# A linear-attention and token-mixer kernel: state packed without its zero blocks, crossbar transposes on another queue and for fewer batches

## The chip, the cores and the metric

The kernel runs on one core of a Trainium2 chip. Five engines take part, each with its own in-order instruction stream: PE (TensorE, matmuls), DVE (VectorE), ACT (ScalarE), POOL (GpSimd) and SP (SyncE, which here only issues transfers). The metric is the device time of one execution in microseconds. Before the change the median of three runs is 233.55 us (233.35 to 233.89).

## The reference, cut to what matters

Batch 4, 8 heads, 768 time steps, head size 48. A gated recurrence gives y, and y, with the heads side by side (384 wide), goes through a token mixer and a channel mixer:

```python
f = 1 / (1 + exp(-f_logit))
for t in range(768):
    state = f[:, :, t, :, None] * state + einsum('bhd,bhe->bhde', k[:, :, t], v[:, :, t])
    y[:, :, t] = einsum('bhd,bhde->bhe', q[:, :, t], state)
x = heads_side_by_side(y)                     # (4, 768, 384)
h = relu(x.T @ w_tok1) @ w_tok2               # over the 768 steps, hidden 256
u = x + h.T
out = u + relu(u @ w_ch1) @ w_ch2             # over the 384 channels, hidden 1536
```

## The kernel before, in words

**Attention.** Each batch b is worked in three blocks d of 256 steps, and each block in two chunks e of 128 steps; below "(b,d)" is one block. The recurrence is done chunk by chunk: within a chunk the sum of log gates is taken by matmuls (`cums`), its exponentials multiply q and k (`gate`, four DVE instructions a block), the gated q and k are transposed so that the head dimension lies on the partitions, `score` forms q times k for 8 heads, `mk` masks it on DVE, `av` multiplies with v, and `qs` adds what q reads from the state of the chunk before. `ds` forms the chunk's contribution to the state (k times v), DVE adds and scales the state (`s_add`, `s_mul`, `s_first`), and POOL casts it to bf16 (`bdc`). Two heads share 128 partitions, at rows 0 to 47 and 64 to 111. Before the change `ds` multiplies both heads of a pair against both v's, so half of each 96-column result is unwanted; DVE and POOL pick the wanted halves with two instructions each, and the bf16 state is a block-diagonal tile with zeros beside each head's block, so that one 128-row matmul of `qs` serves a pair. ACT then copies y out of PSUM (`xev`, L510), POOL or ACT casts it for the mixer.

**Mixing.** Per batch there are 12 matmuls of 384 columns in `tok1`, 12 in `tok2`, 72 in `ch1` (L595) and 72 in `ch2` (L626). ACT and DVE take the results out of PSUM (relu, L606 and L608; additions, L554 and L638), and SP stores the output in two transfers per block.

**Two ways to transpose.** Batch 0 transposes q, k and u with matmuls against an identity (L408, L566) and copies the results out of PSUM on ACT or DVE. Batches 1 to 3 use crossbar transposes by DMA, from SBUF to SBUF, two per block for q and k (L421) and one per block for u (L581). They are issued from ACT's stream.

**What sets the order.** A planner in the kernel (class `Planner`) gives each operation an engine, a cost and a priority, and walks a made-up clock; the engines then run the instructions in the order it found. So an edit of costs or priorities rearranges all five streams. Four PSUM slots (pool "PP", two banks each) are shared by everything that PE writes. Each of f, q, k and v has five load buffers. The transfers that SP and ACT issue share eight completion semaphores in rotation in program order, so a transfer waits until the one that is eight places earlier has ended, whichever queue that one is on. POOL loads the weights; a small POOL write into a load buffer (`gate_w`) holds the loads of batch 1 back until the weights are issued.

Of the kernel before, what the change touches and what calls it, by code (L numbers as in the profile page):

```python
# [11 lines left out]
ALU = mybir.AluOpType  # L12
# [22 lines left out]
class Planner:  # L35
# [23 lines left out]
    def run(self):  # L59
# [25 lines left out]
        free, pipe = {}, 0.0  # L85
        slot_of, last = {}, {}
        order = []
        while ready:
# [27 lines left out]
            if o.xfer is not None and o.xfer < 0:  # L116
                begin = st + occ + 0.5
                end = begin - (2 if pipe > begin else 1) * o.xfer + 1.2
                pipe = max(pipe, begin) - o.xfer
            elif o.xfer is not None:  # L120
                begin = max(st + occ + 0.5, pipe)
                pipe = begin + o.xfer
                end = pipe + 1.2
# [14 lines left out]
            for u, issued in users.get(id(o), []):  # L138
                waiting[id(u)] -= 1
                ready_at[id(u)] = max(ready_at[id(u)], st + occ if issued else end + SEM)  # L140
                if waiting[id(u)] == 0:
                    ready.append(u)
# [12 lines left out]
def kernel(  # L155
# [22 lines left out]
    XB_FROM = 1  # L178
# [40 lines left out]
    bd_tiles = [st([128, HP, 2 * D], BF16, f"state_bd{i}") for i in range(3)]  # L219
# [10 lines left out]
    def consts():  # L230
# [16 lines left out]
        for t in st_tiles + bd_tiles:  # L247
# [3 lines left out]
    LD_ISSUE, ROW = 0.8, 0.019 / 16  # L251
# [21 lines left out]
    def weight(nm, pieces, prio, after):  # L273
# [3 lines left out]
        P.op(nm, {"POOL": (1.2 * len(pieces), 0)}, [], [nm], fn, prio, after, xfer=w_mb[nm] / 0.38)  # L277
# [5 lines left out]
    for kt in range(2):  # L283
        P.value(f"w2s{kt}", f"w2s{kt}", "z")
    P.op("w2l", {"POOL": (2.4, 0)}, [], ["w2s0", "w2s1"], lambda: [nc.gpsimd.dma_start(
        out=P[f"w2s{kt}"], in_=moe_w_tok2[128 * kt:128 * kt + 128]) for kt in range(2)], -898, ["~w1"],
        xfer=w_mb["w2"] / 0.38)
    P.op("w2", {"DVE": (1.0, 0.1)}, ["w2s0", "w2s1"], ["w2"], lambda: [nc.vector.tensor_copy(
        w_tok2[:, kt].rearrange("r c (two p) -> r c p two", two=2),
        P[f"w2s{kt}"].rearrange("r (c p two) -> r c p two", p=64, two=2)) for kt in range(2)], -898)  # L290
    for nm, dst, src, pr, dep in (("wc1", w_ch1, moe_w_ch1, -897, "w2l"),
                                  ("wc2", w_ch2, moe_w_ch2, -896, "wc1")):
# [3 lines left out]
         lambda: nc.gpsimd.memset(P["gw"][0:1, 0, 0, 0:1], 0.0), -895, ["~wc2"])  # L296
# [14 lines left out]
    def attention(b, d):  # L311
        i, pr = f"{b},{d}", 100 * b + 20 * d
# [36 lines left out]
        flex = {"DVE": dve_t(384), "POOL": pool_t(384, True)} if b == 0 else {"POOL": pool_t(384, True)}  # L349
# [35 lines left out]
        def vcast():  # L385
# [4 lines left out]
            nc.gpsimd.tensor_copy(o[64:128, 0], x[0:64, 1])  # L390
            nc.gpsimd.tensor_copy(o[0:64, 2], x[64:128, 0])
        P.op(f"U{i}", {"POOL": (2.5, 0.1)}, [f"v{i}"], [f"U{i}"], vcast, pr + 1)
# [315 lines left out]
```

## Time and profile before

| | before |
|---|---|
| median of the runs | 233.55 us (233.35 to 233.89) |
| the profiled execution | 232.6 us, of which the span in the profile is 230.7 us |
| busy in the span | PE 172.3 us (75%), DVE 145.1 (63%), ACT 90.4 (39%), POOL 84.0 (36%) |
| DMA, share of 16 engines | loads and stores on SP's queue 46.0%, crossbar transposes on ACT's queue 19.2%, weights on POOL's queue 8.1% |
| mean granted PE clock | 0.931 |
| last copy of y out of PSUM (L510) starts, batches 0 to 3 | 44.9, 93.7, 139.9, 181.9 |

Times below are microseconds from the start of the span. A row such as "L454 DVE TENSOR_TENSOR AmT<-pp,msk ... x24 | 28.9, 1220" is a group of instructions: 24 of them, 28.9 us in all, 1220 ns in the mean. [...] A row named "ACTq" or "SPq" is the engine's queue issuing transfers; it does not count as busy.

### The profile page before, as it was taken

What the parts mean: (1) busy time and instruction counts of PE and PEld (TensorE: products, weight loads), DVE (VectorE), ACT (ScalarE), POOL (GpSimd) and SP (SyncE); (2) the same over time, 40 slices, a digit from 0 to 9 for tenths busy, and PEclk for the clock granted to TensorE, in tenths of its full rate; (3) what the DMA queues carried; (4) which work ended last, traced back from release to release, by engine and by line L of the source; (5) the groups of instructions that cost most, each with busy time, mean ns of one, the idle gap of its engine ahead of it and who ended that gap; (6) DMA issues with size and microseconds to landing.
All of it is one profiled execution on the core that took longest, in us unless ns stands there. A gap on an engine that the chain in (4) does not pass through costs nothing.

```text
span 230.7 us, 3882 instructions
## 1 busy us (share of the span) xinstructions
PE 172.3 (75%) x1514; PEld 101.9 (44%) x1514; DVE 145.1 (63%) x221; ACT 90.4 (39%) x130; POOL 84.0 (36%) x134
## 2 busy tenths in 40 slices
PE   0455726585976859948828999929998999799990
PEld 0243424343443435623514556514554656456550
DVE  4699897549893976938837855908876516124211
ACT  4754505286437816423224267211244512244000
POOL 2279942177745286900546626104302101000000
PEclk9999999999795999995965999988999999999998
DMA  7999999999897999979990330693435004711052
GB/s 170 261 261 231 214 203 236 263 260 265 142 257 175 264 207 194 239 120 236 178 230 0 45 49 0 71 183 67 107 81 78 4 0 80 161 24 44 1 138 68
DMA packets 82642, 33.48 MB, mean 145 GB/s; under 512 B 76608, under 2 KB 82240, under 8 KB 82624
## 3 DMA queue, kind: packets, MB, share of 16 engines
q1 hardware_dynamic: 53376, 23.60, 46.0%
q10 hardware_dynamic: 26208, 6.49, 19.2%
q0 software_dynamic: 3040, 3.15, 8.1%
q8 instruction: 12, 0.20, 0.3%
q14 instruction: 6, 0.05, 0.1%
HBM read 25.17 MB, written 4.72 MB: 130 GB/s over the span
## 4 chain that ended last, share of the span: by engine, by line
PE 41%; DVE 19%; DMA 15%; ACT 9%; issue 8%; ACTq 4%; POOL 1%; SPq 0%; DVEq 0%; POOLq 0%
PE pp L595 15%; PE pp L626 12%; DVE qkh L398 7%; DMA qkT<-qkh 6%; DVE AmT L454 4%; ACTq L421 4%; PE pp L548 3%; DMA q_ld<-in_q_dram 3%; DMA out_dram<-xu 3%; PE pp L528 2%; PE pp L451 2%; DVE state L493 2%; DMA uT<-u_bf 2%; ACT xu L510 2%; ACT f_ld L346 2%
## 5 line engine op out<-in xcount | busy, mean ns | idle before, releaser
L595 PE MATMUL pp<-uT,w_ch 128*128 128x384 bf16 x288 | 58.6, 348 | 5.9 <-ACT zT L606 2.2
L626 PE MATMUL pp<-w_ch,zT 128*128 128x384 bf16 x288 | 57.2, 331 | 2.1 <-ACT xu L510 1.9
L595 PEld LDWEIGHTS <-w_ch 128*128 128x128 bf16 x288 | 28.0, 103 | 26.9 <-issue 11.0
L606 ACT ACTIVATE zT<-pp 128x768 bf16<-128x768 f32 x31 | 24.7, 813 | 32.3 <-PE pp L595 27.4
L626 PEld LDWEIGHTS <-zT 128*128 128x128 bf16 x288 | 27.0, 99 | 19.9 <-issue 3.7
L454 DVE TENSOR_TENSOR AmT<-pp,msk 128x1024 bf16<-128x1024 f32 x24 | 28.9, 1220 | 9.7 <-PE pp L451 9.4
L506 POOL CAST state_bd<-state 48x192 bf16<-48x192 f32 x40 | 15.8, 396 | 34.4 <-DVE state L496 27.5
L608 DVE TENSOR_SCALAR zT<-pp 128x768 bf16<-128x768 f32 x17 | 16.3, 957 | 15.3 <-PE pp L595 11.7
L638 DVE TENSOR_TENSOR xu<-xu,pp 128x768 f32<-128x768 f32 x12 | 11.4, 949 | 19.0 <-PE pp L626 19.0
L510 ACT COPY xu<-pp 128x768 f32<-128x768 f32 x12 | 9.6, 799 | 29.2 <-PE pp L469 13.7
L554 DVE TENSOR_TENSOR xu<-xu,pp 128x768 f32<-128x768 f32 x12 | 11.2, 952 | 13.6 <-PE pp L548 13.6
L451 PE MATMUL pp<-qkT 48*128 48x128 bf16 x192 | 10.7, 252 | 10.8 <-ACT xu L510 4.2
L398 DVE TENSOR_TENSOR qkh<-q_ld,G 128x384 bf16<-128x384 f32 x24 | 15.1, 670 | 4.3 <-ACT G L377 4.3
L462 PE MATMUL pp<-v_bf,AmT 128*128 128x48 bf16 x192 | 9.9, 194 | 10.6 <-DVE AmT L454 10.6
L398 DVE TENSOR_TENSOR qkh<-k_ld,Gi 128x384 bf16<-128x384 f32 x24 | 17.7, 776 | 0.0
L302 POOL CAST x_bf<-xu 128x768 bf16<-128x768 f32 x10 | 8.5, 846 | 25.3 <-ACT xu L510 22.6
L548 PE MATMUL pp<-h1T,w_tok 128*128 128x384 bf16 x48 | 12.9, 432 | 4.2 <-ACT h1T L533 4.2
L350 DVE TENSOR_TENSOR Pf<-f_ld 128x384 f32<-128x384 f32 x12 | 9.3, 788 | 9.7 <-ACT f_ld L348 6.4
L528 PE MATMUL pp<-x_bf,w_tok 128*128 128x384 bf16 x48 | 13.3, 372 | 2.8 <-POOL x_bf L302 1.8
L462 PEld LDWEIGHTS <-AmT 128*128 128x128 bf16 x192 | 7.9, 103 | 15.5 <-DVE AmT L454 14.3
L451 PEld LDWEIGHTS <-qkT 48*128 48x128 bf16 x192 | 7.2, 110 | 16.2 <-issue 8.7
L388 POOL CAST v_bf<-v_ld 64x768 bf16<-64x768 f32 x12 | 11.4, 946 | 8.2 <-DMA v_ld<-in_v_dram 4.0
(72 smaller groups left out, 230.4 us busy)
## 6 DMA issues: line engine op xcount, KB each, us to landing
f_ld<-in_f_logit_dram SPq DMA_DIRECT2D x12, 384.0 KB, 6.2
q_ld<-in_q_dram SPq DMA_DIRECT2D x12, 384.0 KB, 6.2
k_ld<-in_k_dram SPq DMA_DIRECT2D x12, 384.0 KB, 6.0
v_ld<-in_v_dram SPq DMA_DIRECT2D x12, 384.0 KB, 6.1
out_dram<-xu SPq DMA_DIRECT2D x24, 192.0 KB, 3.0
w_ch<-in_moe_w_ch_dram POOLq DMA_DIRECT2D x2, 1152.0 KB, 16.8
w_tok<-in_moe_w_tok_dram POOLq DMA_DIRECT2D x2, 192.0 KB, 6.6
zT<-in_moe_w_tok_dram POOLq DMA_DIRECT2D x2, 192.0 KB, 6.6
```

The lines of the kernel that those rows point to most:

```text
L398: nc.vector.tensor_tensor(gated(z, nm, j), x[:, j], gg[:, j], ALU.mult)
L451: nc.tensor.matmul(A[:, par, hp], lhsT=qkT(1, hp, e, rows), rhs=qkT(0, hp, e, rows), start=True, stop=True)
L454: P.op(f"mk{ic}", {"DVE": dve_t(1024)}, [f"A{ic}"], [f"Am{ic}"], lambda ic=ic: nc.vector.tensor_tensor(P[f"Am{ic}"], P[f"A{ic}"].rearrange ...
L462: nc.tensor.matmul(y[:, h], lhsT=P[f"Am{ic}"][:, (h % 2) * 4 + h // 2, :], rhs=vb[:, h], start=(h == 0), stop=(c == 0 and h == H - 1), ski ...
L506: nc.gpsimd.tensor_copy(P[f"bd{ic}"][r, :, cl], P[f"st{ic}"][r])
L510: lambda: nc.scalar.copy(P[f"x{i}"], P[f"yc{b},{2 * d}"][:, :, 0:DM]), pr + 2)
L528: nc.tensor.matmul(pm[:, rt, 0:DM], lhsT=w_tok1[:, kt, rt * 128:(rt + 1) * 128], rhs=P[f"xb{b},{kt // 2}"][:, kt % 2], start=(kt == 0), st ...
L548: nc.tensor.matmul(pm[:, s, 0:DM], lhsT=w_tok2[:, kt, tt, :], rhs=P[f"h1{b}"][:, kt, :], start=(kt == 0), stop=(kt == 1))
L595: nc.tensor.matmul(pm[:, th, 0:384].rearrange("p (a t) -> p a t", t=128), lhsT=w_ch1[:, kt, cc * 128:(cc + 1) * 128], rhs=uT[:, 3 * th:3 * ...
L606: nc.scalar.activation(o, x, AF.Relu)
L608: nc.vector.tensor_scalar(o, x, 0.0, None, ALU.max)
L626: nc.tensor.matmul(pm[:, s, 0:DM], lhsT=P[f"z{b},{cc}"][:, tt * 128:(tt + 1) * 128], rhs=w_ch2[:, cc, :], start=(cc == 0), stop=(cc == NCC ...
```

## The change

- `ds` forms each head by itself: a 64-column half of the gated k against that head's 48 columns of v, its result on the 64 partitions of that head. That makes 32 matmuls a block where there were 16, and a state result without unwanted halves. DVE adds and scales the state with one 128-partition instruction where two of 48 partitions were needed, and POOL casts it with one. The block-diagonal tile and its zeros go.
- `qs` reads the compact state head by head: eight matmuls of 48 rows and 48 columns a chunk where there were four of 128 rows and 96 columns. y lies in PSUM sorted by head parity (one bank for even heads, one for odd), and `xev` puts the heads in order when it copies.
- Batch 1 now transposes on PE as batch 0 does; only batches 2 and 3 use the crossbar. Those transposes are issued from SP instead of ACT.
- The cast of v is split in two operations, and in batch 0 ACT may take the second. In batch 0 the copies of transposed q and k are on ACT alone. The rearranging copy of `w_tok2` (L288) may go to POOL, with a later priority. The second channel weight is loaded only after the first k of batch 1 has arrived (`gate_2`), and the loads of batch 1 no longer wait for its issue.
- The planner's costs for loads, weights and transposes are altered, and attention gets a priority number that is 70 lower, which is earlier. In the new order 342 of the 672 mixer matmuls stand behind the last state read, in the old 255.

**The SP stream at the loads of batch 3.** Names: `qkT` is the transposed pair q and k, `qkh` the gated ones, `xu` the output. Before:

```order
L258 DMA f_ld_73<-in_f_logit_dram 128x8x96
L258 DMA f_ld_72<-in_f_logit_dram 128x8x96
L258 DMA q_ld_77<-in_q_dram 128x8x96
L258 DMA k_ld_82<-in_k_dram 128x8x96
L258 DMA v_ld_90<-in_v_dram 128x8x96
L258 DMA f_ld_75<-in_f_logit_dram 128x8x96
L258 DMA q_ld_79<-in_q_dram 128x8x96
L258 DMA k_ld_84<-in_k_dram 128x8x96
L645 DMA out_dram<-xu_121 64x2x384 x2
```

and now:

```order
L259 DMA f_ld_74<-in_f_logit_dram 128x8x96
L259 DMA f_ld_75<-in_f_logit_dram 128x8x96
L432 DMA_TRANSPOSE qkT_108<-qkh_105 128x16x64 x2
L259 DMA q_ld_79<-in_q_dram 128x8x96
L432 DMA_TRANSPOSE qkT_107<-qkh_106 128x16x64 x2
L259 DMA k_ld_82<-in_k_dram 128x8x96
L654 DMA out_dram<-xu_121 64x2x384 x2
L259 DMA v_ld_89<-in_v_dram 128x8x96
L259 DMA f_ld_72<-in_f_logit_dram 128x8x96
L654 DMA out_dram<-xu_122 64x2x384 x2
```

The transposes of batch 2, each pair waiting for DVE's gated q and k, now stand between the loads of batch 3: ten of the twelve loads come behind the first of them.

**The DVE stream in batch 0**, from the gates of block (0,0) to those of (0,1). Before:

```order
L302 CAST qkT_107<-pp_152 128x2x8x64
L489 TENSOR_TENSOR state_116<-pp_154,glast_113 48x192 x2
L350 TENSOR_TENSOR Pf_92<-f_ld_74 128x384
L372 TENSOR_TENSOR pp_153<-pp_153,f_ld_73 128x384
L454 TENSOR_TENSOR AmT_110<-pp_155,msk 128x1024
L454 TENSOR_TENSOR AmT_111<-pp_152,msk 128x1024
L355 TENSOR_TENSOR Plo_95<-Pf_92,Phi_94 128x8x48
L398 TENSOR_TENSOR qkh_105<-q_ld_78,G_101 128x8x48 x2
```

and now:

```order
L375 TENSOR_TENSOR pp_153<-pp_153,f_ld_73 128x384
L507 TENSOR_TENSOR state_116<-pp_155,glast_113 128x192
L504 TENSOR_TENSOR state_116<-state_116,pp_155 128x192
L507 TENSOR_TENSOR state_116<-state_116,glast_113 128x192
L467 TENSOR_TENSOR AmT_110<-pp_154,msk 128x1024
L467 TENSOR_TENSOR AmT_111<-pp_155,msk 128x1024
L353 TENSOR_TENSOR Pf_92<-f_ld_74 128x384
L408 TENSOR_TENSOR qkh_105<-q_ld_78,G_101 128x8x48 x2
```

The copy of the transposed q has left DVE for ACT, the state of both chunks is done ahead of the masks, and each of its steps is one instruction.

**The ACT stream around the third batch's first mixing step** (`h1T`, the relu of `tok1`). Before:

```order
L379 ACTIVATE Gi_104<-pp_153 128x768
L381 ACTIVATE glast_114<-pp_153 128x8
L421 DMA_TRANSPOSE qkT_107<-qkh_106 128x16x64 x2
L421 DMA_TRANSPOSE qkT_108<-qkh_105 128x16x64 x2
L533 ACTIVATE h1T_132<-pp_154 128x768
L557 CAST u_bf_136<-xu_122 128x768
L581 DMA_TRANSPOSE uT_137<-u_bf_136 128x6x128
```

and now:

```order
L382 ACTIVATE Gi_103<-pp_155 128x768
L542 ACTIVATE h1T_132<-pp_152 128x768
L615 ACTIVATE zT_143<-pp_153 128x768
L517 COPY xu_122<-pp_154 128x2x8x48
L384 ACTIVATE glast_114<-pp_152 128x8
```

No transfer is issued from ACT any more. The core of the diff:

```diff
-            if o.xfer is not None and o.xfer < 0:
-                begin = st + occ + 0.5
-                end = begin - (2 if pipe > begin else 1) * o.xfer + 1.2
-                pipe = max(pipe, begin) - o.xfer
+            if o.xfer is not None and e == "POOL":
+                sw = max(st + occ + 1.5, sw) + o.xfer
+                pipe = max(pipe, st + occ) + o.xfer
+                end = sw + 1.0
             elif o.xfer is not None:
...
+                pipe = max(st + occ + 0.5, pipe) + o.xfer
+                free[e] = max(free[e], pipe - 4.5)
+                end = pipe + 1.0
...
-    XB_FROM = 1
+    XB_FROM = 2
...
-    bd_tiles = [st([128, HP, 2 * D], BF16, f"state_bd{i}") for i in range(3)]
+    bd_tiles = [st([128, HP, D], BF16, f"state_bf{i}") for i in range(3)]
...
-    LD_ISSUE, ROW = 0.8, 0.019 / 16
+    LD_ISSUE, ROW = 1.1, 0.0235 / 16
...
-    P.op("w2", {"DVE": (1.0, 0.1)}, ["w2s0", "w2s1"], ["w2"], lambda: [nc.vector.tensor_copy(
-        w_tok2[:, kt].rearrange("r c (two p) -> r c p two", two=2),
...
+    P.op("w2", {"DVE": (0.6, 0.1), "POOL": (1.6, 0.1)}, ["w2s0", "w2s1"], ["w2"], lambda e: [cast(
+        e, w_tok2[:, kt].rearrange("r c (two p) -> r c p two", two=2),
...
-                                  ("wc2", w_ch2, moe_w_ch2, -896, "wc1")):
+                                  ("wc2", w_ch2, moe_w_ch2, -896, "gate_2")):
...
-         lambda: nc.gpsimd.memset(P["gw"][0:1, 0, 0, 0:1], 0.0), -895, ["~wc2"])
+         lambda: nc.gpsimd.memset(P["gw"][0:1, 0, 0, 0:1], 0.0), -896.5, ["~wc1"])
+    P.op("gate_2", {"POOL": (0.1, 0.1)}, ["k1,0"], [],
+         lambda: nc.gpsimd.tensor_copy(gate_t, P["k1,0"][:, 0, 0, 0:1]), -896.2)
...
-        i, pr = f"{b},{d}", 100 * b + 20 * d
+        i, pr = f"{b},{d}", 100 * b + 20 * d - 70
...
+        P.op(f"V{i}", {"POOL": (1.02, 0.1), "ACT": (0.74, 0.12)} if b == 0 else {"POOL": (1.02, 0.1)}, [f"v{i}"],
+             [f"V{i}"], vshift, pr + 1.5)
...
-                P.op(f"ev{z}{i}", {"ACT": act_t(1024), "DVE": dve_t(1024)}, [f"T{z}{i}"],
+                P.op(f"ev{z}{i}", {"ACT": act_t(1024)} if b == 0 else {"ACT": act_t(1024), "DVE": dve_t(1024)},
...
-                P.op(f"xb_t{i},{e}", {"ACT": (0.8, 0)}, [f"qh{i}", f"kh{i}"], [f"qkT{i},{e}"],
-                     lambda e=e: nc.scalar.dma_start_transpose(
+                P.op(f"xb_t{i},{e}", {"SP": (1.5, 0)}, [f"qh{i}", f"kh{i}"], [f"qkT{i},{e}"],
+                     lambda e=e: nc.sync.dma_start_transpose(
                          P[f"qkT{i}"][:, 1024 * e:1024 * (e + 1)].rearrange("p (n t) -> p n t", t=64),
...
         def ds():
...
-                        nc.tensor.matmul(P[f"dS{i}"][:, e, hp * 2 * D:(hp + 1) * 2 * D], lhsT=kblk(r, j, hp),
-                                         rhs=P[f"U{i}"][r, e + j, hp * 2 * D:(hp + 1) * 2 * D],
-                                         start=(j == 0), stop=(j == 1), skip_group_check=True)
...
+                        kb = kblk(r, j, hp)
+                        for par in range(2):
+                            h = 2 * hp + par
+                            nc.tensor.matmul(P[f"dS{i}"][64 * par:64 * par + 64, e, hp * D:(hp + 1) * D],
+                                             lhsT=kb[:, 64 * par:64 * par + 64],
+                                             rhs=P[f"U{i}"][r, e + j, h * D:(h + 1) * D],
+                                             start=(j == 0), stop=(j == 1), skip_group_check=True)
...
+            def yv(h, e=e, ic=ic):
+                o = e * HP * D + (h // 2) * D
+                return P[f"ya{ic}"][:, h % 2, o:o + D]
...
-                for hp in range(HP):
-                    nc.tensor.matmul(y[:, hp], lhsT=qkT(0, hp, e), rhs=bd[:, hp, :],
-                                     start=False, stop=(hp == HP - 1), skip_group_check=True)
...
+                s_ = P[f"bd{b},{c - 1}"]
+                for h in range(H):
+                    hp, r = h // 2, slice(64 * (h % 2), 64 * (h % 2) + D)
+                    nc.tensor.matmul(yv(h), lhsT=qkT(0, hp, e, r), rhs=s_[r, hp, :], start=False, stop=True,
+                                     skip_group_check=True)
...
             def s_add(ic=ic, dsv=dsv):
-                for r, cl in half:
-                    nc.vector.tensor_tensor(P[f"st{ic}"][r], P[f"st{ic}"][r], dsv()[r, :, cl], ALU.add)
...
+                nc.vector.tensor_tensor(P[f"st{ic}"], P[f"st{ic}"], dsv(), ALU.add)
...
-                for r, cl in half:
-                    nc.gpsimd.tensor_copy(P[f"bd{ic}"][r, :, cl], P[f"st{ic}"][r])
...
+            P.op(f"bd{ic}", {"POOL": (0.36, 0.1)}, [f"st{ic}"], [f"bd{ic}"],
+                 lambda ic=ic: nc.gpsimd.tensor_copy(P[f"bd{ic}"], P[f"st{ic}"]), pr + 1)
...
-                P.op(f"uT{i}", {"ACT": (1.0, 0)}, [f"ub{i}"], [f"uT{i}"],
-                     lambda i=i, p=p: nc.scalar.dma_start_transpose(
+                P.op(f"uT{i}", {"SP": (1.5, 0)}, [f"ub{i}"], [f"uT{i}"],
+                     lambda i=i, p=p: nc.sync.dma_start_transpose(
```

76 lines of the change are left out of this document (35 added, 41 removed).

## The prediction

> **What bounds the kernel now.** I read the busy time by stretches first, then the chain of waits, then single streams. The stretches end about where the attention of each batch ends (the table above has when the last copy of y out of PSUM starts):
>
> ```profile
> core 0: us, PE busy (x) PEld busy (x) DVE busy (x) ACT busy (x) POOL busy (x), PEclk, DMA share, GB/s
> 3.00:45.00 42.00, 22.32 (x250) 15.15 (x250) 33.81 (x51) 17.41 (x26) 21.44 (x31) 1.00 1.24 241
> 45.00:94.00 49.00, 37.18 (x341) 20.41 (x341) 36.59 (x52) 30.96 (x47) 30.92 (x45) 0.90 1.10 218
> 94.00:140.00 46.00, 35.49 (x321) 20.70 (x320) 30.38 (x45) 16.39 (x25) 18.92 (x29) 0.81 0.67 133
> 140.00:182.00 42.00, 35.84 (x353) 21.04 (x351) 28.45 (x45) 13.90 (x22) 9.50 (x19) 0.96 0.46 81
> ...
> 182.00:231.00 49.00, 41.51 (x254) 24.55 (x252) 14.06 (x15) 10.43 (x13) 1.66 (x2) 0.98 0.26 61
> ...
> sum 179.00, PE 130.83 PEld 77.29 DVE 129.23 ACT 78.67 POOL 80.78; mean PE 32.71 PEld 19.32 DVE 32.31 ACT 19.67 POOL 20.20
> ```
>
> (The last row sums the first four.) DVE is the busiest in the first stretch (33.81 of 42 us, 80%), 75% in the second, 66% and 68% in the third and fourth; PE's time in the later ones is swollen by a granted clock of 0.81 to 0.96. No engine is full: what paces these 179 us is handing work from engine to engine, with DVE's work (129.2 us, 72%) as the nearest floor. What interrupts the handing on is in the chain:
>
> ```profile
> 80.54 8.19 DMA qkT<-qkh
> 107.16 5.27 DMA qkT<-qkh
> 212.97 11.71 PE pp L626 x72
> 224.78 0.95 DVE xu L638
> ```
>
> Crossbar transposes stand in it for 8.19 and 5.27 us at a time. The last two rows show another regime: after the attention, PE runs dense matmuls at 11.71 / 72 = 0.163 us each, and 6.0 us pass between its end (224.68) and the span's end at 230.7. ACT's own stream shows what issuing the transposes costs, before the third batch's relu of the token mixer:
>
> ```profile
> 145.47 7.67 ACTq L421 DMA_TRANSPOSE qkT<-qkh  x4
> 153.18 0.81 ACT L533 ACTIVATE h1T<-pp 128x768 bf16<-128x768 f32 x1 [7.68 <-issue]
> L421 ACTq DMA_TRANSPOSE qkT<-qkh x18: 1257/1758/3676, 57.6 to 172.7; - x18
> L581 ACTq DMA_TRANSPOSE uT<-u_bf x9: 1225/1228/2539, 111.3 to 194.9; - x9
> ```
>
> ACT stands for 7.68 us while four transposes are issued; at the medians the 27 take 18 x 1.758 + 9 x 1.228 = 43 us of its stream, beside its 90.4 us of work. And SP's loads wait for those transposes through the shared completion semaphores:
>
> ```profile
> SPq L258 <- DMA qkT<-qkh: 27.2, 5, 7.5
> q10 hardware_dynamic: 26208, 6.49, 19.2%
> ```
>
> 27.2 us in five waits; and the transposes' queue fills 16 engines for 19.2% of 230.7, 44 us.
>
> **The change, term by term.** The end is the time at which DVE gets through the last mask of the attention, then the last state read, then the dense matmuls behind it, then the tail. On DVE, and for what ACT takes over:
>
> ```profile
> L454 DVE TENSOR_TENSOR AmT<-pp,msk 128x1024 bf16<-128x1024 f32 x24 | 28.9, 1220 | 9.7 <-PE pp L451 9.4
> L608 DVE TENSOR_SCALAR zT<-pp 128x768 bf16<-128x768 f32 x17 | 16.3, 957 | 15.3 <-PE pp L595 11.7 <-ACT xu L510 3.5
> L638 DVE TENSOR_TENSOR xu<-xu,pp 128x768 f32<-128x768 f32 x12 | 11.4, 949 | 19.0 <-PE pp L626 19.0
> L493 DVE TENSOR_TENSOR state<-state,pp 48x192 f32<-48x192 f32 x32 | 11.2, 349 | 3.5 <-PE pp L430 1.8 <-POOL state_bd L506 1.0
> L496 DVE TENSOR_TENSOR state<-state,glast 128x192 f32<-128x192 f32 x16 | 6.6, 413 | 0.3
> L489 DVE TENSOR_TENSOR state<-pp,glast 48x192 f32<-48x192 f32 x8 | 2.8, 352 | 0.9 <-PE pp L430 0.7
> L288 DVE COPY w_tok<-zT 128x768 bf16<-128x768 bf16 x2 | 4.4, 2388 | 0.0
> L302 DVE CAST qkT<-pp 128x1024 bf16<-128x1024 f32 x3 | 3.7, 1220 | 1.5 <-PE pp L408 1.5
> 179.32 1.23 DVE L454 TENSOR_TENSOR AmT<-pp,msk 128x1024 bf16<-128x1024 f32 x1
> L300 ACT CAST qkT<-pp 128x1024 bf16<-128x1024 f32 x3 | 3.0, 1012 | 11.1 <-PE pp L408 11.1
> L606 ACT ACTIVATE zT<-pp 128x768 bf16<-128x768 f32 x31 | 24.7, 813 | 32.3 <-PE pp L595 27.4 <-DVE pp L372 4.6 <-PE pp L626 0.3
> ```
>
> - State: 56 instructions, 11.2 + 6.6 + 2.8 = 20.6 us, become 36 of 128x192. The 48-row ones have the same 192 elements on a partition and take 0.349, the 128-row ones 0.413 in the mean; I take 0.35 (the two of the first kind are one each now), 12.6 us: -8.0 (bound -5.7).
> - The copy of `w_tok2` goes to POOL: -4.4.
> - Casts of transposed q and k: three before, two now: -1.2.
> - Relus on DVE: 17 before, 9 now, ACT takes the others: -8 x 0.957 = -7.7. Copies of transposed u: one before, two now, +0.95.
>
> Together -20.3. Behind the last mask stood 14.1 us of DVE's work (the row from 182 on); in the new order 13 instructions of some 0.95 stand there, 12.4 us. So DVE has 129.2 - 20.3 + 1.7 = 110.6 us to do up to its last mask.
>
> How fast it gets through: 72% over the 179 us. I take 75%, the share of the second stretch. For a higher one: the first stretch had 80%; ACT loses 43 us of issuing and does some 14 us more work (eight relus of 0.81, seven casts of about 1.0, smaller pieces both ways), so 133 us of its stream become about 105; batch 1's transposes cost a few us on PE and ACT instead of landing times. For a lower one: the leaner DVE leaves more of the pace to the others, and PE gets more to do. Both ends go into the range: 70% and 82%.
>
> PE's additions, from its stream among dense matmuls:
>
> ```profile
> 111.44 0.52 PE L430 MATMUL pp<-v_bf,qkh 64*128 64x96 bf16 x16
> 111.89 0.66 PE L626 MATMUL pp<-w_ch,zT 128*128 128x384 bf16 x3
> 163.90 0.33 PE L469 MATMUL pp<-state_bd,qkT 128*128 128x96 bf16 x4
> 164.07 0.65 PE L626 MATMUL pp<-w_ch,zT 128*128 128x384 bf16 x3
> 159.23 0.40 PE L451 MATMUL pp<-qkT 48*128 48x128 bf16 x8
> 159.56 1.15 PE L626 MATMUL pp<-w_ch,zT 128*128 128x384 bf16 x6
> 165.48 0.33 PE L362 MATMUL pp<-Phi,tri 128*128 128x384 bf16 x1
> 166.01 0.65 PE L626 MATMUL pp<-w_ch,zT 128*128 128x384 bf16 x3
> 162.17 0.36 PE L462 MATMUL pp<-v_bf,AmT 128*128 128x48 bf16 x8
> 162.37 0.65 PE L626 MATMUL pp<-w_ch,zT 128*128 128x384 bf16 x3
> L430 PEld LDWEIGHTS <-qkh 64*128 64x128 bf16 x192 | 5.4, 103 | 8.1 <-DVE qkh L398 6.0 <-issue 1.8 <-DVE state L489 0.3
> ```
>
> Sixteen `ds` matmuls cost 111.89 - 111.44 = 0.45 us, 28 ns each; four `qs` cost 0.17; eight 48-column `av` cost 0.20, 25 ns each; eight `score` 0.33; a block's `cums` 0.53. A 64x64 tile with 48 columns was never run, so I bound it: nothing added if four tiles overlap fully; 32 x 28 ns = 0.9 us, +0.45 a block, if each is issued like a present one; 32 x 103 ns = 3.3 us, +2.85, if each waits for its whole weight load. I take +0.45, the row it is nearest to. `qs`: eight at 25 ns and 0.2 for entering and leaving the half-height array (0.09 us passes between two dense matmuls and the 111.44 row) is 0.4, +0.23 for each of 20. Twelve blocks and 20 reads: 5.4 + 4.6 = 10 us. Batch 1's 66 transposes (48 of q and k, 18 of u) have a third of a dense matmul's columns, 0.054 us each: 3.6.
>
> Up to the last state read PE then has 330 mixer matmuls (counted in the new order) at 0.163, 53.7 us; the attention as it was, 12 x (0.45 + 2 x 0.33 + 2 x 0.20 + 0.53) + 20 x 0.17 + 3.6 for batch 0's transposes = 31.5; and these 13.6. That is 98.8 us from its first matmuls at about 8, 69% of the time that DVE sets. Covered; with the upper bound it isn't (rival 2).
>
> POOL loses half of its 40 casts of state, some 8 us, and gains the `w_tok2` copy: between 2 x 0.85 us (its cast of x, as many elements) and the 2 x 2.39 that DVE took; it lies in the first stretch, where POOL is busy for half the time, and costs up to 3 us if a state cast waits behind it. SP gets the transposes: see the first rival.
>
> **The sum.** 3.0 (start of the stretch) + 110.6 / 0.75 = 147.5, so the last mask ends at 150.5 instead of 180.6 (the row at 179.32). The last state read follows 1.1 us later, as before. Behind it stand 342 mixer matmuls in the new order, 255 in the old (attention has moved ahead of them): 342 x 0.1626 = 55.6. Tail 6.0. Span 213.2. The same sum for the kernel before, 180.6 + 1.1 + 41.5 + 6.0 = 229.2, is 1.5 short of 230.7, so the method is good to a few us. The median of the runs is 233.55, 2.85 above the profiled span: **216 us**.
>
> **Rivals.**
> 1. *Transposes queue behind loads on SP.* Now ten of batch 3's twelve loads come behind batch 2's first transposes, and these wait for DVE's gates. Each block of batch 2 may have to let the loads ahead of it land, and PE, which runs in order, stands for it. A load's median to landing:
>
> ```profile
> q_ld<-in_q_dram SPq DMA_DIRECT2D x12, 384.0 KB, 6.2
> ```
>
>    Three blocks: 18.6 us, span 231.8, time 234.7, about the old time. For it: the 27.2 us above show that SP's waits were already of that kind. Against it: the transfers need no longer be shared with batch 1's transposes (a third of 44 us), and in the new order the gates of (2,0) stand 16 rows of DVE ahead of the mask that needs their transposes.
> 2. *Column tiles are slow, the change is slower.* With 103 ns for each `ds` pair and 103 for each `qs` pair, PE gets 12 x 2.85 + 20 x 0.65 = 47 us instead of 10, so 136 us up to the last state read. At 80% that is 8 + 170 = 178, plus 55.6 and 6.0: 239.6, time 242.5. It decides once PE's work passes 0.8 x 143 = 115 us, that is some 70 ns for a `ds` pair. Against it: the 25 to 28 ns rows, where weight loads of 103 ns overlap freely.
>    [...] No run so far shows a column tile. [...]
> 3. *Everything flows.* Without ACT's stalls PE's clock stays full and DVE reaches 82%: 3.0 + 134.9 + 62.7 = 200.6, time 203.5. For it: PE's low clock follows its stalls. Against it: even the first stretch, without crossbar or mixer, had 80%.
>
> **How the numbers follow.** The forecast has 0.64; its own range goes from 82% to 70% of DVE, 203 to 226. Rival 1 has 0.16 (spread around the old time), rival 2 0.10, rival 3 0.10. The range takes in the forecast, rival 1's lower two thirds and half of rival 3: 203 to 233. A measurement of this kernel can tell about 0.2%, 0.5 us. Faster: 0.64 + 0.10 + 0.4 x 0.16 = 0.80; within 0.2%: 0.03; slower 0.17.
>
> **What would show it.** Last copy of y of batch 0 near 38 and of batch 3 near 151 instead of 44.9 and 181.9; DVE busy some 125 us in all; `ds` with 32 matmuls in about 0.9 us among dense ones; no transposes on ACT; about 62 us between the last state read and the end. Wrong: SP waits in front of transposes with PE idle behind them (rival 1), `ds` at 2 us or more (rival 2), or a DVE share below 66%.

## The result

The changed kernel takes 210.78 us in the median of four runs (209.39 to 211.04); the kernel before took 233.72 beside it (233.35 to 235.90). The ratio is 0.8989, with a 95% interval of 0.8921 to 0.9057: faster, by 23 us. The forecast was 216.0, the range 203 to 233. The profiled execution took 211.04 us, its span is 209.3.

The page of the changed kernel: busy time of the engines, one row of its queues, and the chain's shares by engine.

```profile
PE 168.3 (80%) x1852; PEld 103.4 (49%) x1852; DVE 128.6 (61%) x188; ACT 104.5 (50%) x147; POOL 80.5 (38%) x117
...
q1 hardware_dynamic: 70848, 27.93, 65.3%
...
PE 54%; DVE 27%; ACT 8%; issue 6%; DMA 2%; POOL 1%; DVEq 0%; POOLq 0%; ACTq 0%
```

Transfers held 15% of the chain before and ACT's queue 4%; now it is 2% and nothing. The transposes share one queue (q1) with the loads. The table of stretches of the changed kernel (columns as in the prediction; 147.70 is where the last state read starts):

```profile
3.00:147.70 144.70, 112.39 (x1506) 69.76 (x1507) 114.63 (x161) 81.47 (x119) 76.39 (x104) 0.96 0.96 189
147.70:209.00 61.30, 55.90 (x351) 33.49 (x350) 12.24 (x13) 21.70 (x27) 2.48 (x3) 0.98 0.28 62
...
3.00:41.40 38.40, 22.09 (x318) 14.34 (x318) 28.36 (x38) 20.44 (x31) 20.49 (x24) 1.00 1.17 239
41.40:79.70 38.30, 30.40 (x420) 19.37 (x420) 29.81 (x45) 29.98 (x44) 21.05 (x30) 0.96 0.97 195
79.70:105.20 25.50, 19.94 (x263) 12.27 (x261) 23.84 (x31) 11.45 (x19) 19.28 (x28) 0.97 0.95 195
105.20:123.30 18.10, 15.60 (x190) 9.32 (x189) 13.87 (x20) 8.69 (x14) 8.62 (x13) 0.85 1.00 188
123.30:148.00 24.70, 24.66 (x326) 14.69 (x325) 18.76 (x27) 11.19 (x17) 6.95 (x11) 1.00 0.61 94
```

DVE does 114.63 us of work in 144.70, 79% (before 129.23 in 178.6, 72%). PE is full from 123.3 on (24.66 of 24.70); before that it stands for 32 of 120.3 us. Of the marks that the prediction named: batch 0's last copy of y starts at 41.40 (38 foreseen), the last state read of batch 3 is over at 147.85 (the copy of y behind it, foreseen near 151, starts at 154.67, since ACT's copy before it waits 9.2 us for a store to free its buffer, and ACT then waits 5.5 us more for an addition on DVE; PE has no gap from that), DVE is busy for 128.6 us (some 125), and 61.5 us lie between the last state read and the end (62).

Single streams of the changed kernel on PE: a block's chunk states (`ds`, L444) and the last state reads (L485) among dense matmuls.

```profile
130.92 0.44 PE L444 MATMUL pp<-v_bf,qkh 64*64 64x48 bf16 x32
131.29 1.39 PE L557 MATMUL pp<-h1T,w_tok 128*128 128x384 bf16 x7
...
147.35 0.36 PE L478 MATMUL pp<-v_bf,AmT 128*128 128x48 bf16 x8
147.65 0.27 PE L485 MATMUL pp<-state_bf,qkT 48*128 48x48 bf16 x8
147.85 4.40 PE L635 MATMUL pp<-w_ch,zT 128*128 128x384 bf16 x26
```

Thirty-two column-tiled matmuls (64 rows by 64 columns each) take 131.29 - 130.92 = 0.37 us from their row's start to the next row's (the row's own 0.44 runs into the next), 12 ns each; the sixteen before took 0.45. Eight `av` and eight `qs` take 0.30 + 0.20, where eight `av` and four `qs` took 0.20 + 0.17.

And one place where the change costs something: the rearranging copies of the second token weight on POOL, DVE beside them, and the gates by group, with what PE waited for them.

```profile
27.64 7.05 POOL L305 COPY w_tok<-zT 128x768 bf16<-128x768 bf16 x2
...
27.11 2.36 DVE L467 TENSOR_TENSOR AmT<-pp,msk 128x1024 bf16<-128x1024 f32 x2
29.39 0.34 DVE L504 TENSOR_TENSOR state<-state,pp 128x192 f32<-128x192 f32 x1
29.65 4.83 DVE L408 TENSOR_TENSOR qkh<-k_ld,Gi 128x384 bf16<-128x384 f32 x2
...
L408 DVE TENSOR_TENSOR qkh<-k_ld,Gi x24: 543/773/3515, 11.9 to 137.9; 128x384 bf16<-128x384 f32 x24
...
PE pp L444 <- DVE qkh L408: 4.9, 4, 3.1
```

Two gates take 4.83 us, one of them 3.515 instead of 0.773 (the median); the masks in the same window keep their 1.18. PE stands 3.1 us for that gate, the longest of its four such waits.

### The profile page after: what moved, and what is told of

It is laid out like the page before. It is cut to its first block, busy times and chain, and to the rows that moved or that the text cites. A ratio compares the mean times of both kernels' runs of the same rounds, so it can differ in the third digit from the quotient of the medians.

```text
span 209.3 us, 4507 instructions
## 1 busy us (share of the span) xinstructions
PE 168.3 (80%) x1852; PEld 103.4 (49%) x1852; DVE 128.6 (61%) x188; ACT 104.5 (50%) x147; POOL 80.5 (38%) x117
## 4 chain that ended last, share of the span: by engine, by line
PE 54%; DVE 27%; ACT 8%; issue 6%; DMA 2%; POOL 1%; DVEq 0%; POOLq 0%; ACTq 0%
PE pp L635 20%; PE pp L604 18%; DVE qkh L408 11%; DVE AmT L467 5%; PE pp L537 3%; PE pp L557 3%; ACT G L380 2%; DVE Pf L353 2%; DVE state L507 2%; DMA f_ld<-in_f_logit_dram 2%; PE pp L478 2%; PE pp L464 2%; PE pp L418 1%; PE pp L444 1%; DVE xu L563 1%
## 5 line engine op out<-in xcount | busy, mean ns | idle before, releaser
L604 PE MATMUL pp<-uT,w_ch 128*128 128x384 bf16 x288 | 51.7, 330 | 1.6 <-ACT Gi L382 0.8
L635 PE MATMUL pp<-w_ch,zT 128*128 128x384 bf16 x288 | 51.6, 333 | 0.4 <-DVE xu L563 0.4
L615 ACT ACTIVATE zT<-pp 128x768 bf16<-128x768 f32 x39 | 31.5, 812 | 27.9 <-DVE xu L647 17.3
L408 DVE TENSOR_TENSOR qkh<-k_ld,Gi 128x384 bf16<-128x384 f32 x24 | 21.3, 926 | 0.0
L517 ACT COPY xu<-pp 128x768 f32<-128x768 f32 x12 | 9.5, 795 | 21.8 <-PE pp L485 12.6
L408 DVE TENSOR_TENSOR qkh<-q_ld,G 128x384 bf16<-128x384 f32 x24 | 17.3, 759 | 1.9 <-ACT G L380 1.8
L514 POOL CAST state_bf<-state 128x192 bf16<-128x192 f32 x20 | 7.8, 388 | 27.1 <-DVE state L507 27.0
L418 PE MATMUL pp<-ident,qkh 128*128 128x128 bf16 x96 | 10.5, 264 | 4.4 <-DVE qkh L408 3.8
L380 ACT ACTIVATE G<-pp 128x768 bf16<-128x768 f32 x12 | 9.8, 813 | 6.9 <-DVE pp L375 6.9
L303 ACT CAST qkT<-pp 128x1024 bf16<-128x1024 f32 x10 | 10.1, 1010 | 5.5 <-PE pp L418 5.5
L444 PE MATMUL pp<-v_bf,qkh 64*64 64x48 bf16 x384 | 6.4, 199 | 7.0 <-DVE qkh L408 4.9
L305 POOL CAST v_bf<-v_ld 64x384 bf16<-64x384 f32 x20 | 11.6, 579 | 1.0
```

Of the source, the lines that this page charges most:

```text
L305: (nc.vector if e == "DVE" else nc.gpsimd).tensor_copy(o, x)
L380: P.op(f"G{i}", {"ACT": act_t(768)}, [f"S{i}", f"S1{i}"], [f"G{i}"], lambda: nc.scalar.activation(P[f"G{i}"], sv(), AF.Exp, bias=0.0, scal ...
L408: nc.vector.tensor_tensor(gated(z, nm, j), x[:, j], gg[:, j], ALU.mult)
L418: nc.tensor.matmul(P[f"T{z}{i}"][:, n // 4, (n % 4) * 128:(n % 4 + 1) * 128], lhsT=P[f"{nm}{i}"][:, m * 128:(m + 1) * 128], rhs=ident, sta ...
L604: nc.tensor.matmul(pm[:, th, 0:384].rearrange("p (a t) -> p a t", t=128), lhsT=w_ch1[:, kt, cc * 128:(cc + 1) * 128], rhs=uT[:, 3 * th:3 * ...
L615: nc.scalar.activation(o, x, AF.Relu)
```

## Experiments

After the result I set three theories against each other. *Handing on*: ACT's stream freed of issuing, and batch 1 off the crossbar, let DVE run at 79%. *Order*: the gain is the attention's earlier place in the streams. *Less work*: it is the compact state and the shorter DVE list. Where a run says "streams ordered anew", the planner made a new order from the edit, so its difference holds the new order as well; runs 1, 3, 10, 11 and 12 keep the order of all engines but for what they move. Differences between runs are of medians unless a ratio is named; each ratio is to the kernel before beside that run.

**1. Transposes back on ACT, order kept.**

```
- lambda e=e: nc.sync.dma_start_transpose(       + lambda e=e: nc.scalar.dma_start_transpose(
- lambda i=i, p=p: nc.sync.dma_start_transpose(  + lambda i=i, p=p: nc.scalar.dma_start_transpose(
```

> The changed kernel with every engine's order kept, and the crossbar transposes of batches 2 and 3 issued from ACT's stream again instead of SP's; nothing else differs. Handing on (my theory: freeing ACT of issuing, and batch 1 of the crossbar, raised DVE's share from 0.72 to 0.79): 18 transposes (12 of q and k, 6 of u) cost ACT 12 x 1.76 + 6 x 1.23 = 28 us of its stream, a quarter of it or more shows: 216 to 221 us. Order (rival: the gain is that attention stands earlier in the streams; the queue is worth little): 210 to 213. Less work (rival: compact state and fewer DVE instructions are the gain): 210 to 213.

Measured 216.35 us, ratio 0.9234 (0.9165 to 0.9303): 5.6 us slower than the changed kernel, as handing on expects. What it looks like on ACT, in the timeline of this run:

```profile
85.25 0.81 ACT L380 ACTIVATE G<-pp 128x768 bf16<-128x768 f32 x1 [1.56 <-DVE pp L375]
85.25 1.34 ACTq L432 DMA_TRANSPOSE qkT<-qkh  x1
86.64 0.81 ACT L382 ACTIVATE Gi<-pp 128x768 bf16<-128x768 f32 x1 [0.58 <-ACT G L380]
86.66 1.78 ACTq L432 DMA_TRANSPOSE qkT<-qkh  x1
88.48 0.84 ACT L349 ACTIVATE f_ld<-f_ld 128x768 f32<-128x768 f32 x1 [1.04 <-issue]
```

Between two activations that could follow each other stands a transpose's issue: ACT idles for 0.58 and 1.04 us, and what waits for `Gi` comes later. In the changed kernel the same activations stand close:

```profile
86.50 0.81 ACT L380 ACTIVATE G<-pp 128x768 bf16<-128x768 f32 x1 [1.57 <-DVE pp L375]
87.20 0.80 ACT L382 ACTIVATE Gi<-pp 128x768 bf16<-128x768 f32 x1
87.89 0.84 ACT L349 ACTIVATE f_ld<-f_ld 128x768 f32<-128x768 f32 x1
```

From the first start to the third it takes 1.39 us there and 3.23 here. The transposes of q and k land about as fast from either queue (4.9 us in the median here, 4.6 there). How such delays add up to 5.6 us was not followed.

**2. Batch 1 on the crossbar too, from SP; streams ordered anew.**

```
- XB_FROM = 2
+ XB_FROM = 1
```

> The changed kernel with batch 1 on the crossbar too (transposes from SP's queue), the streams ordered anew for that. Handing on: nine transposes more behind SP's loads, landing times of 4 to 5 us in batch 1's chain, DVE's share back to some 0.75: 218 to 221 us. Order and less work: PE saves 66 transposes (3.6 us) and ACT and DVE six copies: 208 to 212.

211.62 us, ratio 0.9023 (0.8973 to 0.9073): no difference from the changed kernel that could be told. Handing on had expected 218 to 221, the other two theories 208 to 212; moving batch 1 to PE is worth nothing that could be told once SP issues.

**3. That same order, all 27 transposes from ACT.**

```
- nc.sync.dma_start_transpose(     (both places, in the kernel of run 2)
+ nc.scalar.dma_start_transpose(
```

> The order of the run with batch 1 on the crossbar, kept as it is, with all 27 transposes issued from ACT. So both halves of the change to the transposes are undone. Moving the queue back alone cost 5.6 us for 18 transposes; batch 1 on the crossbar alone cost 0.8 at most. Handing on (ACT's stream is what matters): 27 transposes hold it, of which nine stand in the densest third: 211.6 + 27/18 x 5.6 = 220 us, or more where both compound, 218 to 224. Order (the queue's cost belongs to one unlucky place in that order): 212 to 216. Loads behind transposes (a rival formed now: 27 us of SP's waits for transposes in the kernel before are the lost time, and come back when many transposes share the DMA engines with the loads): 224 or more, and SP shows waits for transposes again.

220.73 us, ratio 0.9422 (0.9376 to 0.9468): 9.1 us above run 2, close to 27/18 of run 1's 5.6. With ACT issuing, batch 1 on the crossbar costs some 4 us (against run 1); from SP it costs none. So the issuing queue is what matters, and batch 1's place matters only with it. What the queue does, though, is more than one thing here. ACT's stream is held, as in run 1, and the transposes of q and k land later: 5.7 us in the median and 9.1 at most, against 4.3 and 6.6 in run 2. The chain of run 2 has no transpose in it; in that of run 3 they stand for 25 us, in these rows:

```profile
60.52 8.05 DMA qkT<-qkh
101.80 6.99 DMA qkT<-qkh
118.06 6.39 DMA qkT<-qkh
156.54 3.78 DMA qkT<-qkh
```

Besides the very first load, three loads stand in that chain too, for 16 us; in run 2's it is one, for 4.9. Which of this costs the 9 us was not separated. SP waits 3.2 us for transposes in this run (27.2 in the kernel before), so loads behind transposes are at most a part of it.

**4. The block-diagonal state, streams ordered anew.** The lines of the change on `bd_tiles`, `ds`, `av`, `qs`, the state on DVE, its cast and the copy of y are taken back, the rest stays:

```
- bd_tiles = [st([128, HP, D], BF16, f"state_bf{i}") for i in range(3)]
+ bd_tiles = [st([128, HP, 2 * D], BF16, f"state_bd{i}") for i in range(3)]
...
- nc.vector.tensor_tensor(P[f"st{ic}"], P[f"st{ic}"], dsv(), ALU.add)
+ for r, cl in half:
+     nc.vector.tensor_tensor(P[f"st{ic}"][r], P[f"st{ic}"][r], dsv()[r, :, cl], ALU.add)
...
```

> The changed kernel with the block-diagonal state of the kernel before: 16 matmuls for the chunk states, 4 for the state reads, 56 DVE instructions on the state instead of 36, two POOL casts each. Streams ordered anew. Handing on: DVE gets 7 to 8 us back, through 0.79 that is 9 to 10 us, less 1 to 2 us of PE: 218 to 221 us. Less work: most of the 23 us of gain goes: 224 to 230. Order: 212 to 215.

213.62 us, ratio 0.9114 (0.9062 to 0.9167): 3 us, not the 10 that DVE's work over its share gives. Its stretch up to the last state read:

```profile
3.00:149.40 146.40, 111.77 (x1237) 70.27 (x1237) 121.52 (x180) 85.16 (x125) 86.18 (x122) 0.93 0.93 185
```

DVE has 6.9 us more to do and does it in 1.7 us more: its share goes from 79% to 83%. A share that rises when work is added is not a rate. The time lies in the range that the theory of order had given, 212 to 215, and outside those of the other two.

**5. No priority offset; streams ordered anew.**

```
- i, pr = f"{b},{d}", 100 * b + 20 * d - 70
+ i, pr = f"{b},{d}", 100 * b + 20 * d
```

> The changed kernel without the offset of 70 in the planner's priorities that puts a batch's attention ahead of the previous batches' mixer. The order of all streams is planned anew from that; instructions are the same. Order: most of the gain goes, 222 us or more. Handing on and less work: the dense matmuls move from behind the attention into it, PE still has room there: 212 to 218.

212.06 us, ratio 0.9044 (0.8998 to 0.9091), an interval that overlaps the changed kernel's. The two stretches, with the last state read at 167.5 instead of 147.7:

```profile
3.00:167.50 164.50, 132.67 (x1629) 82.13 (x1630) 115.30 (x165) 90.92 (x130) 75.63 (x105) 0.94 0.86 171
167.50:210.00 42.50, 36.08 (x228) 21.45 (x227) 10.23 (x11) 12.20 (x15) 0.83 (x1) 0.99 0.29 70
```

The attention ends 20 us later and the kernel 1 us later: 123 fewer matmuls stand behind it. The theory of order, which had expected 222 or more, falls. None of the three has all of runs 1, 2, 4 and 5 in its ranges: handing on has runs 1 and 5, less work runs 2 and 5, order runs 2 and 4.

**6. The old order of the weights' loads; streams ordered anew.**

```
- ("wc2", w_ch2, moe_w_ch2, -896, "gate_2")      + ("wc2", w_ch2, moe_w_ch2, -896, "wc1")
- ... P["gw"] ..., -896.5, ["~wc1"])             + ... P["gw"] ..., -895, ["~wc2"])
- P.op("gate_2", ...)
```

> The changed kernel with the old order of the loads of weights: the second channel matrix is issued right behind the first, and batch 1's first load waits for that, instead of the other way round. Streams ordered anew. Handing on: batch 1's loads come some 3 us later (1.2 MB at the rate of the stretch), DVE has batch 0 to do meanwhile: 211 to 213 us. Loads (the order of transfers in the first 60 us was the larger gain): 217 or more.

212.70 us, ratio 0.9071 (0.9032 to 0.9110): 1.9 us in the median, and the intervals overlap.

One at a time, the parts of runs 1, 2, 4, 5 and 6 are worth 5.7 + 0.8 + 2.9 + 1.3 + 1.9 = 12.6 us (differences of ratios to 0.8989, times 234). Of these, runs 2, 5 and 6 overlap the changed kernel in their intervals. So half of the 23 was missing, and the next runs look for it.

**7. All five undone at once; streams ordered anew**, the transposes on ACT with the planner's knowledge (`{"SP": (1.5, 0)}` becomes `{"ACT": (1.5, 0)}`); the diffs are those of 1, 2, 4, 5 and 6 together.

> The changed kernel with five parts undone: block-diagonal state, transposes of batches 1 to 3 from ACT (known to the planner), no priority offset, old order of the weights. What stays is the planner's cost model, the copy of the token weight on POOL or DVE, and the split of the cast of v. If the gain is the sum of the parts undone: 210.8 + 5.6 + 0.8 + 2.5 + 1 + the loads' share = 221 to 225. If they compound (each covers for the other): 228 to 234, the old time. If the planner's model is most of it: under 219.

234.78 us, ratio 1.0007 (0.9969 to 1.0044): the old time. The parts compound in the sense of the forecast (with one part missing the others cover for it), and what was left in (the planner's costs, the token weight's copy, the split cast of v, batch 0's copies on ACT alone) brings nothing in sum. SP's waits in this run:

```profile
SPq L259 <- DMA qkT<-qkh: 13.4, 3, 7.4
SPq L259 <- DMA uT<-u_bf: 6.2, 2, 5.9
```

The loads' waits for transposes are back, 20 us where the kernel before had 27 for `qkT` alone.

**8. Of these five, only the queue put back; streams ordered anew** (27 transposes from SP; block-diagonal state, crossbar for batch 1, old priorities and loads stay).

> The run with five parts undone, of which one is put back: the 27 transposes of batches 1 to 3 go from SP (and the planner knows it). Four parts stay undone. If the parts compound around the transposes (each transpose that waits on a stream makes the other parts dear): most of the 24 us comes back, 215 to 222 us. If the queue is worth the same wherever it is (5.6 us in the changed kernel, 7.2 in the kernel before): 227 to 230. If no one part of the five carries it: above 230.

217.35 us, ratio 0.9290 (0.9245 to 0.9335): 17.4 of the 24 us (16.8 by the ratios). The same move with the order kept, run 10 below, is worth 7.3, so this figure holds what the planner makes of it.

**9. Of these five, only the compact state put back; streams ordered anew** (transposes stay on ACT).

> The run with five parts undone, of which another one is put back: the compact state. Transposes of batches 1 to 3 stay on ACT. By my prediction's rule (DVE's work divided by its share): 8.0 us less on DVE at 0.71 is 11 us, 223 to 225. By what the changed kernel showed for the same part (2.5 us, DVE's share gave way and PE's work stayed): 231 to 233. If the streams compound, 226 to 230.

222.85 us, ratio 0.9554 (0.9503 to 0.9604): 11.9 us (10.6 by the ratios). Up to the last state read, runs 7, 8 and 9, one row each:

```profile
3.00:186.90 183.90, 135.81 (x1315) 82.09 (x1315) 130.73 (x193) 80.31 (x117) 85.55 (x124) 0.87 0.85 167
```

```profile
3.00:171.60 168.60, 128.89 (x1276) 78.32 (x1276) 122.23 (x185) 87.98 (x126) 83.17 (x122) 0.86 0.92 180
```

```profile
3.00:178.30 175.30, 132.42 (x1570) 80.00 (x1569) 126.27 (x174) 77.70 (x114) 77.56 (x103) 0.91 0.92 173
```

DVE's share is 71, 72 and 72%. Run 9's time is within 0.2 us of what my rule gives (223 to 225), but not by its way: DVE has 4.5 us less up to there, not 8, since the new order gave it other work; 4.5 / 0.72 is 6 of the 8.6 us by which the last state read moves. The rest, and what happens behind it, I put down to the new order; that was not followed.

**10. The kernel before in its own order, transposes from SP.**

```
- nc.scalar.dma_start_transpose(     (both places)
+ nc.sync.dma_start_transpose(
```

> The kernel before, in its own order, with its 27 transposes issued from SP's stream instead of ACT's; nothing else differs. Handing on: ACT gets 43 us of its stream back, but transposes that wait for the gates now stand before loads in an order planned without them: a gain of 3 to 10 us, 224 to 231. Loads behind transposes: SP waits longer still, no gain or a loss: 232 to 240. Order: within 2 us of the old time.

227.15 us, ratio 0.9688 (0.9647 to 0.9729): 7.3 us faster (by the ratio) from the move of the queue alone, although PE stands for the transposes longer here than in any other run (a row of PE's waits):

```profile
PE pp L451 <- DMA qkT<-qkh: 15.5, 4, 9.5
```

So what rival 1 describes does exist, where the order was planned without it: 9.5 us at one place. In the changed kernel's order it is gone.

**11. The token weight's copies on ACT, at the same place, order kept.**

```
- cast(e, w_tok2[:, kt].rearrange("r c (two p) -> r c p two", two=2),
+ cast("ACT", w_tok2[:, kt].rearrange("r c (two p) -> r c p two", two=2),
```

> The changed kernel in its own order, with the two rearranging copies of the second token weight issued on ACT instead of POOL, at the same place in the order; nothing else differs. There they took 7.05 us on POOL, and a gate on DVE beside them took 3.5 us instead of 0.8, on the path. ACT stands idle for 3.49 us at that place and for 3.81 a little later. If the collision on memory is what made the gate slow and ACT's copies do not do the same: the gates come back to 1.6 us for two, batch 0 ends 2 to 3.5 us earlier, and the end follows: 207 to 209 us. If the front's gain is lost again before the PE-bound rest: 210 to 211. If ACT is as slow on the rearranging copy as POOL: 211 to 214.

210.90 us, ratio 0.8994 (0.8946 to 0.9042): the same as the changed kernel (the profiled execution was the fastest of six, 208.16, with a granted clock of 0.98). The timelines of ACT and DVE say why:

```profile
26.73 7.09 ACT L303 COPY w_tok<-zT 128x768 bf16<-128x768 bf16 x2
33.30 1.16 ACT L517 COPY xu<-pp 128x768 f32<-128x768 f32 x1
...
29.67 1.02 DVE L408 TENSOR_TENSOR qkh<-k_ld,Gi 128x384 bf16<-128x384 f32 x2
```

ACT takes as long as POOL (7.09 us), but the gates beside it take 1.02 instead of 4.83: what slowed them goes with the copy on POOL (7.05 us), not with the copy's traffic as such. Part of the gain is lost at once, because a copy of y (30.34 in the changed kernel) now stands behind the second copy until 33.30, and batch 0's last one starts at 40.72 instead of 41.40.

**12. The two copies in two pauses of ACT, order kept otherwise.**

```
  (one copy, kt = 0, at the place of run 11)
  def ev(e, z=z):
      ...
+     if b == 0 and d == NP - 1 and z == 1:
+         cast("ACT", w_tok2[:, 1].rearrange("r c (two p) -> r c p two", two=2),
+              P["w2s1"].rearrange("r (c p two) -> r c p two", p=64, two=2))
```

> The changed kernel in its own order, with the first of the two rearranging copies on ACT where POOL had both, and the second on ACT behind the last cast of transposed k of batch 0; nothing else differs. With both at the first place the gates took 1.02 us for two instead of 4.83, but the two copies (7.09 us) held a copy of y and two casts for 2.7 us, and batch 0 ended 0.7 us earlier only. Now each copy stands in a pause of ACT as long as it is (3.5 us): batch 0's last copy of y starts near 38.2 instead of 41.4. If batch 0's end carries over: 3 us less, 207 to 208.5. If batch 1's loads or PE's work behind it take the 3 us up: 209.5 to 211.

208.15 us (206.28 to 208.72 in six runs), ratio 0.8880 (0.8837 to 0.8923). All six lie below the lowest of the changed kernel's four (209.39); against the same kernel before on each chip it is 1.1% better, with intervals that touch. ACT's timeline:

```profile
26.70 3.67 ACT L303 COPY w_tok<-zT 128x768 bf16<-128x768 bf16 x1
30.33 0.80 ACT L520 COPY xu<-pp 128x768 f32<-128x768 f32 x1
...
33.78 3.63 ACT L303 COPY w_tok<-zT 128x768 bf16<-128x768 bf16 x1
37.53 0.80 ACT L520 COPY xu<-pp 128x768 f32<-128x768 f32 x1
```

Batch 0's last copy of y starts at 37.53 instead of 41.40, and the median is 2.6 us lower; with intervals that touch, how much of the 3.9 us reaches the end is not settled closer than that.

## Why the prediction came out, and where its steps did not

**What the time consists of.** The parts of the change are worth 24 us together, 12.6 taken from the changed kernel one by one, and 17.4 for the queue and 11.9 for the state when added to the old arrangement alone. PE's own account reads more plainly: the span is PE's busy time and its standing. That is bookkeeping, true of any engine; it says where the time lies, not why.

| kernel (run) | span | PE busy | PE stands | DVE's share up to the last state read |
|---|---|---|---|---|
| before | 230.7 | 172.3 | 58.4 | 72% |
| five undone (7) | 233.3 | 171.4 | 61.9 | 71% |
| before, transposes on SP (10) | 225.2 | 167.7 | 57.5 | 74% |
| five undone but the state (9) | 220.8 | 168.1 | 52.7 | 72% |
| batch 1 on the crossbar, on ACT (3) | 218.7 | 172.0 | 46.7 | 68% |
| five undone but the queue (8) | 216.0 | 167.6 | 48.4 | 72% |
| transposes on ACT (1) | 214.6 | 170.7 | 43.9 | 78% |
| old state (4) | 211.3 | 167.6 | 43.7 | 83% |
| no offset (5) | 210.3 | 168.7 | 41.6 | 70% |
| old loads (6) | 210.3 | 171.7 | 38.6 | 79% |
| batch 1 on the crossbar, on SP (2) | 209.7 | 167.4 | 42.3 | 75% |
| the change | 209.3 | 168.3 | 41.0 | 79% |
| copies on ACT at one place (11) | 206.4 | 167.2 | 39.2 | 79% |
| copies in ACT's pauses (12) | 206.6 | 170.2 | 36.4 | 78% |

PE's work is 167 to 172 everywhere; what varies is its standing, 62 to 36 us. (The rows are single executions; those of 11 and 12 have granted clocks of 0.98 and 0.93.) DVE's share does not order these kernels: those with 70% and 83% have spans within 2 us of the change's. My reading is that every part shortens the standing ahead of the point from which PE is full, 123 us in the changed kernel, and that there is less of it left to shorten the more parts are in. That the parts compete for the same gaps fits all rows, but it is not shown; which gap each one closes was not followed through the reordered streams.

**The base of the sum** held, as it must when the measured work and share are put in: 3.0 + 114.63 / 0.792 = 147.7, the last state read 0.2 long, 342 dense matmuls from 147.85 to 203.6 (55.75 us; 55.6 foreseen), tail 5.7 (6.0). But two errors partly cancelled in it. DVE had 4.0 us more to do than the 110.6, and got through it at 79% instead of 75%: +5.3 and -8.1 us. The runs took 1.5 us more than the span, not 2.85. So that 216 came within 5 us of 210.8 is in part luck. (Taken to the last mask itself, the sum's own end point, it is 3.0 + 114.63 / 0.798 = 146.7, where 150.5 was foreseen, and the read follows after 0.9 us instead of 1.1. The 72% of the kernel before had been taken up to 182 and not up to its last mask at 180.6, where it is 73%.) As an account of the last execution the sum is right; as a cause it is not: run 4 adds 6.9 us to DVE for 1.7, and run 5 moves the attention's end by 20 us for 1.

**DVE's terms.** State: 36 instructions in 5.5 + 7.4 = 12.9 us (12.6 foreseen). Relus: 9 in 8.6, as counted. The missing 4 us are the gates, 17.3 + 21.3 = 38.6 us where they had 32.8, less 1.8 us on the pairwise sums of log gates (`Pf`, 7.5 instead of 9.3). Of the gates' 5.8 us, 3.6 are gone in run 12 (17.5 + 17.5), where no copy stands on POOL; the other 2.2 have no cause shown.

**The copy on POOL** is the step that failed: "between 2 x 0.85 us and the 2 x 2.39 that DVE took", "up to 3 us if a state cast waits behind it". It took 7.05, outside these bounds, and its harm was not on POOL but on DVE's gates, on the path. Run 12, without that, has batch 0's last copy of y at 37.53, near the 38 that was predicted. The trace of before had shown the two engines in each other's way, at the same place, with the roles exchanged (DVE's copy, and POOL's casts ahead of it and beside it):

```profile
26.20 4.37 DVE L288 COPY w_tok<-zT 128x768 bf16<-128x768 bf16 x2
...
24.39 0.50 POOL L391 CAST v_bf<-v_ld 64x384 bf16<-64x384 f32 x1
26.69 2.12 POOL L390 CAST v_bf<-v_ld 64x384 bf16<-64x384 f32 x1
```

Casts that take 0.50 us took 2.12 and 2.08 beside it. I had read the copy's own duration and not who stood next to it. In the changed kernel the gate that met the second copy has both operands in SBUF; it took 3.515 us and ended at 34.5, just ahead of that copy (3.838 us, from 30.9 to 34.7). The masks, with one operand in PSUM, kept 1.18, and beside ACT's copy of the same data (run 11) two gates took 1.02. By what the two engines get in each other's way was not shown.

**PE's additions** were put at 10 us and are 1.6: `ds` needs 0.08 us a block less than before instead of 0.45 more (the lower bound, nothing added, was the nearest), and `av` with `qs` 0.13 more per read instead of 0.23: 20 x 0.13 - 12 x 0.08. This takes one place among dense matmuls for each, as the prediction did. No run shows the 0.2 us for entering and leaving the half-height array by itself: the eight `qs` cost 0.20 in all, the eight `av` ahead of them 0.30 instead of 0.20. Rival 2 is out: a `ds` pair costs 12 ns, where PE would have decided from some 70.

**ACT.** 104.5 us of work against some 105 foreseen, no transposes on it. That the issuing queue matters is the step that runs 1, 3 and 10 bear out with the order kept: 5.6, 9.1 and 7.3 us for 18, 27 and 27 transposes. It was in the prediction as a reason for a higher share without a price of its own, and it is the largest single part of those tried in either surrounding. The 43 us of issuing that the prediction took off ACT's stream were not 43 us of standing: in the kernel before, ACT's waits that are put down to issuing alone are 7.7, 7.0 and 5.0 us, 19.7 in all, and in run 10 there is none. Run 10 also has the transposes of q and k land sooner, 5.2 us at most where the kernel before had 8.2. So the queue is shown as the cause, and how its worth divides between ACT's stream and the transfers' landing is open.

**Rival 1**, transposes behind loads on SP, did not come. SP waits and PE hardly does (first row: the waits of SP in the changed kernel; the others: who waited for its transposes, and their landing):

```profile
SPq L432 <- DVE qkh L408: 12.9, 3, 6.6
```

```profile
  PEld L464: 1.0, 3
...
DMA to landing us min/median/max: 3.8/4.6/5.3
```

Run 10 shows that it was a real danger: 15.5 us of PE's standing in an order that was not planned for it. **Rival 3**'s 82% was nearer to the share than 75%, for a reason that it didn't name: PE's clock was 0.96, not full, up to the last state read, and by runs 4 and 5 the share is no limit. Of PE's low clock following its stalls, the trace of before shows this much: PE did nothing from 101 to 104 us and its clock was 0.50 from 104 to 110, nothing from 150 to 154 and 0.50 from 155 to 157; yet from 28 to 32 PE was busy for 1.01 us and the clock was 1.00.

## What to carry to other kernels

Read the time of a kernel with one nearly full in-order engine as that engine's work plus its standing, and look for the waits that an edit removes; here the busy share of another engine was no rate to divide by, and the worths of the parts did not add up. Issuing a crossbar transpose held its queue for 1.2 to 3.7 us in the kernel before, so let it come from a queue on which nothing that computes is waiting, and plan the order for that. Before moving a long copy to an engine, look at what runs beside it: here two gates on DVE took 4.83 us beside POOL's copies and 1.02 beside ACT's.

## What was not expected of the hardware

- A gate on DVE, both operands in SBUF, that met a long POOL copy ended about when it did (34.5 and 34.7): the shortest of these gates takes 0.54 us, this one took 3.515 beside a copy of 3.838. The other way round, POOL's casts took 2.12 and 2.08 us instead of 0.50 beside DVE copies of 2.24 and 2.54.
- The rearranging copy of 768 two-byte elements per partition took 2.39 us on DVE, 3.65 on ACT and 3.74 on POOL (the means of two each, those on DVE and POOL beside work of the other); in the changed kernel ACT and POOL cast as many elements of x in 0.83.
- Thirty-two 64x64 tiles with 48 columns passed in 0.37 us among dense matmuls, 12 ns each, though a weight load of such a tile is shown with 118 ns in the mean.
